# Recurrence and gated FFN on one core: weights converted without their range handling, and the range counted in a second pass

## The chip, the cores and the metric

The kernel runs on one core of one Trainium2 chip. The metric is device time in microseconds (us), from one launch. Five engines work side by side, each through its own list of instructions in order: TensorE (PE in the profile; its weight loads are PEld), VectorE (DVE), ScalarE (ACT), GpSimd (POOL) and SyncE (SP, which here only issues DMAs). Waits between engines are semaphores.

## The reference

A linear recurrence over 768 time steps for 4 batches and 8 heads of width 48, followed by a two-layer FFN over the resulting 3072 tokens of width 384. The gate is mish, written as `h * tanh(log1p(exp(h)))`.

```python
for t in range(S):                                   # r, k, v: (4, 8, 768, 48); w, u: (8, 48)
    cur = einsum('bhd,bhe->bhde', u[None] * k[:, :, t], v[:, :, t])
    y[:, :, t] = einsum('bhd,bhde->bhe', r[:, :, t], state + cur)
    state = w[None, :, :, None] * state + einsum('bhd,bhe->bhde', k[:, :, t], v[:, :, t])
x = y.transpose(0, 2, 1, 3).reshape(B * S, H * D)    # (3072, 384)
h = x @ w_in                                         # (384, 2048)
out = (h * tanh(log1p(exp(min(h, 20))))) @ w_out     # (2048, 384)
```

`w_in` and `w_out` arrive as float64, all else as float32. [...]

## The kernel before

**Stages.** Time is cut into 6 chunks of 128 steps; a chunk of one batch is a *step* s (24 steps, four for each chunk). For each step `scale` multiplies r and k by powers of the decay, `scores` (L476) makes the products of a chunk in the PSUM pair `pa`, `attend` (L495) masks them into `P` with a copy under a predicate, and `outputs` makes y (L510, L512 for the first chunk, L527 and L536 later) and the next state. `diag` makes the diagonal of P first (L452 on ACT or L454 on DVE). In the first chunk `keys` (L466) multiplies k by the table `TKn`, and L560 copies a part of v into `pre` for y.

The four steps of a chunk together feed one *group* g of the FFN: 512 tokens, 16 up tiles of 128 features (`hp`), the gate, and 16 down tiles that add into `acc`. The down tile n comes LAG = 6 tiles behind the up tile n. Tiles are numbered through all groups, n = 0 to 95. Group 0 multiplies in plain float32 (L791 for its first four up tiles in pieces of one step each, L716 for the other up tiles, L760 for the down tiles; three matmuls a tile). Groups 1 to 5 use weights and activations that are split in two parts (`w`, nine matmuls a tile, L694). An up tile leaves PSUM by a copy on DVE or ACT (L832 `hb`), two PSUM buffers `hp` take turns. For each pair of tiles ACT runs three activations with two table loads (L727, L730, L733), DVE multiplies (L738, L740), and L744 and L748 split the result.

**Weights.** There are 16 chunks of 768 weights a partition: eight of `w_in` (two up tiles each), eight of `w_out` (two down tiles each), in the order `W_ORDER` in which group 0 needs them: in 0 to 3, out 0, in 4, out 1, in 5, out 2, in 6 and so on. `load_weights` loads each as 768 KB of float64 (tile `wraw`) through POOL's queue. `convert(c)` turns it in place into float32: `up` and `low` are the two halves; the exponent is moved over by shifting `up` left by 3 (L316) after its sign is cleared (L308 on ACT, or L310 on DVE) and the value is clamped into the exponents that the shift can take (L312); the low half becomes a correction (L314 on ACT); the sign is put back (L318); the two are added (L320). `split(c)` (L333, L335) later makes the two parts for groups 1 to 5. Buffers of raw chunks and of parts share 17 slots (`W_SLOTS`).

**What sets the order.** `Flow` plans the whole program before it is emitted: each thread (`convert`, `gate`, `ffn` and so on) yields the events that it needs and the cost of its next instruction for each engine that could take it; `run` takes the one that is ready first, by rank. So the list of each engine is fixed by the planner's costs; where a thread yields costs for two engines (`hb`, `gh`, `diag`), the planner also chooses the engine. `check_range` counts the decays `w` that lie in the range that the kernel is made for, and the last lines load that count: if one is outside, a general path (slow, not run with these inputs) computes all again.

Of the kernel before, what the change touches and what calls it, by code (L numbers as in the profile page):

```python
# [36 lines left out]
E_LO, E_HI = (float(np.array([n], np.uint32).view(np.float32)[0]) for n in (896 << 20, (1151 << 20) - 1))  # L37
# [23 lines left out]
N_SQ = 4  # L61
N_ACT_DIAG = 8
# [74 lines left out]
def dve(cols, fast=False):  # L137
    return {"dve": 0.14 + cols / (1900 if fast else 950)}
# [6 lines left out]
def pe(us):  # L145
    return {"pe": us}
# [3 lines left out]
def rwkv_mish_kernel(ctx, tc, rkT, rkN, vN, wT, w_in, w_out, consts, rkF, vF, wF, uF, outT):  # L150
# [10 lines left out]
    small = const.tile([128, 4 * NP + 4], F32, name="small")  # L161
    wt, wc, iw, inr = (small[:, n * NP : (n + 1) * NP] for n in range(4))
    bias_ln2, early, ones = (small[:, 4 * NP + n : 4 * NP + n + 1] for n in range(3))
    ok = small[0:32, 4 * NP + 3 :].bitcast(I32)
# [100 lines left out]
    def check_range():  # L265
        yield "TKn"
        yield "state3"
        yield {"pool": 0.1}
        nc.gpsimd.memset(ones, 1.0)
        yield dve(NP)  # L270
        nc.vector.tensor_tensor(out=inr, in0=wc, in1=wt, op=ALU.is_equal)
        yield pe(0.1)
        t = ps.tile([128, 512], F32, name="ok", tag="acc2")
        nc.tensor.matmul(t[:32, :NP], lhsT=ones.broadcast_to([128, 32]), rhs=inr, start=True, stop=True)
        yield dve(NP)
        nc.vector.tensor_reduce(out=inr[:32, 0:1], in_=t[:32, :NP], axis=AX.X, op=ALU.add)
        yield dve(1)
        nc.vector.tensor_copy(ok, inr[:32, 0:1])
        flow.set("checked")
# [5 lines left out]

    def load_weights():
        for c, (i, f) in enumerate(W_ORDER):
            yield {"pool": 1.2}
            raws[c] = raw = wpool.tile([128, WE, 2], U32, name="wraw", tag="w")
            nc.gpsimd.dma_start(raw, (w_in, w_out)[i][f].bitcast(U32).rearrange("p (n two) -> p n two", two=2))  # L290
            flow.set(f"issued{c}")

    def convert(c):
# [10 lines left out]
        engine = yield {**dve(WE, True), **act(WE)}  # L304
        e = stage.tile([128, WE], F32, name="we", tag="we", bufs=2)
        eu = e.bitcast(U32)
        if engine == "act":
            nc.scalar.activation(e, up.bitcast(F32), AF.Abs)  # L308
        else:
            v.tensor_scalar(out=eu, in0=up, scalar1=0x7FFFFFFF, scalar2=None, op0=ALU.bitwise_and)  # L310
        yield dve(WE, True)
        v.tensor_scalar(out=e, in0=e, scalar1=E_LO, scalar2=E_HI, op0=ALU.max, op1=ALU.min)  # L312
# [770 lines left out]
```

## Time and profile before

| | |
|---|---|
| three timed runs | 523.43, 523.54, 521.80 us; median 523.43 |
| profiled execution | 521.48 us; span of its instructions 519.7 us |
| mean granted TensorE clock | 0.982 |
| busy share of the span | PE 96%, ACT 78%, DVE 72%, POOL 2% |
| DMA | 46.27 MB, 89 GB/s on average |

PE has hardly any time left over the whole span, but the three stages differ. Up to about 50 us the DMA queues are full with inputs and weights; from there to about 160 us group 0 runs, the weights are converted and split, and DVE and ACT are nearly as busy as PE; after that PE leads by a wide margin until about 512 us. The times of a line in the timeline are the start from the span's start and the duration; in the timeline each float32 matmul shows as two records, so six records are one tile of group 0. Next to a time in brackets stands how long the engine had been idle and what ended it; "issue" there means that the profile shows nothing that was waited for.

### The profile page before, as it was taken

The numbers are of one execution on the slowest core, as the hardware profiler recorded it, in microseconds if no ns is written. First come the engines' busy times: TensorE is split into PE (matmuls) and PEld (weight loads), VectorE is DVE, ScalarE is ACT, GpSimd is POOL, SyncE is SP. The second block draws the span as 40 slices with busy tenths as digits, with TensorE's granted clock in tenths as the row PEclk, the third lists the DMA queues.
The fourth block names the chain that finished last, engine by engine and source line by source line (L and its number), as shares of the span: only waits on it lengthen the run. The fifth ranks groups of instructions, "written<-read, shape, count | busy, mean of one in ns | idle before, by whom it ended". The sixth has DMA issues, their size and how long they took to land. (4 is left out here: it accounts for less than half of the span.)

```text
span 519.7 us, 8994 instructions
## 1 busy us (share of the span) xinstructions
PE 498.7 (96%) x3654; PEld 384.6 (74%) x3654; DVE 373.9 (72%) x582; ACT 404.1 (78%) x504; POOL 10.7 (2%) x25
## 2 busy tenths in 40 slices
PE   6988997999999999999999999999999999999994
PEld 4777462555658888887888888888888888888883
DVE  4949997999988897677966478857488545546551
ACT  2945999789987898876797987887978869769660
POOL 5110000000000000000000000000000000000000
PEclk8789998999999999999999999999999999999999
DMA  8999332211114312013412124321123000010001
GB/s 267 324 365 368 135 115 74 88 61 42 37 50 138 113 41 63 20 67 110 140 44 58 30 73 131 105 66 36 53 78 119 1 6 11 1 61 1 0 1 66
DMA packets 17138, 46.27 MB, mean 89 GB/s; under 512 B 2817, under 2 KB 3329, under 8 KB 17089
## 3 DMA queue, kind: packets, MB, share of 16 engines
q1 hardware_dynamic: 12048, 27.93, 17.8%
q0 software_dynamic: 2304, 12.58, 6.8%
q10 hardware_dynamic: 2736, 5.10, 2.7%
q8 instruction: 31, 0.51, 0.4%
q14 instruction: 19, 0.15, 0.1%
HBM read 38.92 MB, written 4.72 MB: 84 GB/s over the span
## 5 line engine op out<-in xcount | busy, mean ns | idle before, releaser
L694 PE MATMUL hp<-x,w 128*128 128x512 f32 x720 | 181.0, 396 | 0.8 <-DVE hb L832 0.6
L694 PE MATMUL acc<-gh,w 128*128 128x512 f32 x480 | 159.8, 389 | 0.0
L694 PEld LDWEIGHTS hp<-x,w 128*128 128x128 f32 x720 | 133.7, 188 | 32.4 <-issue 1.6
L694 PEld LDWEIGHTS acc<-gh,w 128*128 128x128 f32 x480 | 90.1, 188 | 18.8
L694 PE MATMUL acc<-gl,w 128*128 128x512 f32 x240 | 93.4, 389 | 0.0
L832 DVE COPY hb<-hp 128x512 f32<-128x512 f32 x48 | 33.1, 690 | 55.5 <-PE hp L694 51.3
L740 DVE TENSOR_TENSOR hb<-hb,fa 128x1024 f32<-128x1024 f32 x40 | 48.7, 1219 | 27.4 <-ACT fa L733 27.3
L727 ACT ACTIVATE fa<-hb,small 128x1024 f32<-128x1024 f32 x48 | 55.3, 1152 | 13.9 <-DVE hb L740 13.5
L727 ACT ACT_TABLE_LOAD x48 | 61.6, 1283 | 5.5 <-DVE hb L740 3.7
L733 ACT ACT_TABLE_LOAD x48 | 61.6, 1283 | 0.9
L694 PEld LDWEIGHTS acc<-gl,w 128*128 128x128 f32 x240 | 45.0, 188 | 9.4
L730 ACT ACTIVATE fa<-fa 128x1024 f32<-128x1024 f32 x48 | 50.9, 1060 | 1.0
L733 ACT ACTIVATE fa<-fa 128x1024 f32<-128x1024 f32 x48 | 50.9, 1060 | 0.5
L748 DVE TENSOR_TENSOR gl<-hb,gh 128x1024 fp32r<-128x1024 f32 x40 | 48.8, 1220 | 1.6 <-ACT gh L744 1.2
L832 ACT COPY hb<-hp 128x512 f32<-128x512 f32 x48 | 28.0, 583 | 22.3 <-PE hp L694 18.7
L760 PE MATMUL acc<-gf,wraw 128*128 128x512 f32 x96 | 44.0, 594 | 0.0
L716 PE MATMUL hp<-x,wraw 128*128 128x512 f32 x72 | 35.2, 627 | 3.7 <-issue 3.7
L495 DVE COPY_PREDICATED P<-cst,pa 128x512 f32<-128x512 uint32 x48 | 34.9, 728 | 3.2 <-PE pa L476 2.4
L744 ACT CAST gh<-hb 128x1024 fp32r<-128x1024 f32 x18 | 18.9, 1052 | 19.8 <-DVE hb L740 19.1
L760 PEld LDWEIGHTS acc<-gf,wraw 128*128 128x128 f32 x96 | 18.7, 196 | 19.2 <-issue 18.1
L402 DVE TENSOR_TENSOR rk<-rk,TRK 112x512 f32<-112x512 f32 x44 | 30.0, 683 | 0.0
L716 PEld LDWEIGHTS hp<-x,wraw 128*128 128x128 f32 x72 | 14.0, 201 | 19.4 <-issue 19.1
(101 smaller groups left out, 529.0 us busy)
## 6 DMA issues: line engine op xcount, KB each, us to landing
rk<-in_rkT_dram SPq DMA_DIRECT2D x22, 448.0 KB, 4.0
rkn<-in_rkN_dram SPq DMA_DIRECT2D x20, 384.0 KB, 3.8
wraw<-in_w_in_dram POOLq DMA_DIRECT2D x8, 768.0 KB, 21.7
wraw<-in_w_out_dram POOLq DMA_DIRECT2D x8, 768.0 KB, 23.0
v<-in_vN_dram SPq DMA_DIRECT2D x22, 256.0 KB, 4.0
out_dram<-ob ACTq DMA_DIRECT2D x18, 256.0 KB, 2.2
x<-st SPq DMA_DIRECT2D x60, 32.0 KB, 1.9
rkx<-in_rkT_dram SPq DMA_DIRECT2D x2, 448.0 KB, 16.7
```

The source lines that it names most:

```text
L402: nc.vector.tensor_tensor(out=rk[:112, a], in0=rk[:112, a], in1=TRK[:112, a], op=ALU.mult)
L495: nc.vector.copy_predicated(out=Ps[s][:, :, i].rearrange("j (w z) i -> j w z i", w=2), mask=masks.unsqueeze(2).broadcast_to([128, 2, NP // ...
L694: nc.tensor.matmul(out, lhsT=a, rhs=m, start=first and n == 0, stop=last and n == 2)
L716: nc.tensor.matmul(hp[:, :T], lhsT=e[:, fs], rhs=o.x[:, k, :, 0], start=k == 0, stop=k == KT - 1)
L727: nc.scalar.activation(o.g, o.hb, AF.Sigmoid, bias=bias_ln2, scale=1.0)
L730: nc.scalar.activation(o.g, o.g, AF.Arctan)
L733: nc.scalar.activation(o.g, o.g, AF.Sin, scale=2.0)
L740: nc.vector.tensor_tensor(out=o.hb, in0=o.hb, in1=o.g, op=ALU.mult)
L744: (nc.scalar.copy if engine == "act" else nc.vector.tensor_copy)(out=o.gh, in_=o.hb)
L748: nc.vector.tensor_tensor(out=o.gl, in0=o.hb, in1=o.gh.bitcast(F32), op=ALU.subtract)
L760: nc.tensor.matmul(a, lhsT=whole[1, f // WG][:, ws], rhs=o.gf[:, j], start=f == 0, stop=f == NF - 1)
L832: (nc.scalar.copy if engine == "act" else nc.vector.tensor_copy)(out=o.hb[:, j], in_=h)
```

## The change

`convert` loses its first two instructions: the sign is no longer cleared ahead of the shift (the shift by 3 pushes it out) and the clamp is gone. The shift (now at line 347) reads `up` of the raw chunk. What the clamp guarded is counted later: `check_range` starts after the last split, loads all 16 chunks a second time through SP's queue into the one free slot of the weight buffers, one every three up tiles from tile 44 on, squares the upper half on ACT with a sum (L291), takes the smallest square on DVE (L293), and folds both into `flags`. The one matmul that counts all flags moves from group 0 to just after up tile 92 and takes an `hp` buffer. The first down tile no longer waits for `checked`. The general path converts the weights anew with the clamp. Nothing is changed in what the kernel returns.

```diff
     def check_range():
-        yield "TKn"
-        yield "state3"
+        v = nc.vector
+        yield "w1,%d" % (NW - 1)
         yield {"pool": 0.1}
         nc.gpsimd.memset(ones, 1.0)
+        for c, (i, f) in enumerate(W_ORDER):
+            yield f"u{CHECK_AT + CHECK_STEP * c}"
+            yield {"sp": 2.0}
+            if not c:
+                raw = wpool.tile([128, WE, 2], U32, name="wraw", tag="w")
+            nc.sync.dma_start(raw, weights(c))
+            yield act(WE)
+            e = stage.tile([128, WE], F32, name="we", tag="we", bufs=2)
+            to = more if c else flags
+            nc.scalar.activation(e, raw[:, :, 1].bitcast(F32), AF.Square, accum_out=to[:, 1:2])
+            yield dve(WE)
+            v.tensor_reduce(out=to[:, 0:1], in_=e, axis=AX.X, op=ALU.min)
+            if c:
+                yield {"dve": 0.3}
+                for k, op in enumerate((ALU.min, ALU.add)):
+                    v.tensor_tensor(out=flags[:, k : k + 1], in0=flags[:, k : k + 1], in1=to[:, k : k + 1], op=op)
...
+        yield from hp_free()
+        yield pe(0.3)
+        yield from hp_free(0.0)
+        t = hp_tile("ok", "counted")
+        nc.tensor.matmul(t[:32, :N_FLAGS], lhsT=ones.broadcast_to([128, 32]), rhs=flags, start=True, stop=True)
...
     def convert(c):
...
-        engine = yield {**dve(WE, True), **act(WE)}
-        e = stage.tile([128, WE], F32, name="we", tag="we", bufs=2)
-        eu = e.bitcast(U32)
-        if engine == "act":
-            nc.scalar.activation(e, up.bitcast(F32), AF.Abs)
-        else:
-            v.tensor_scalar(out=eu, in0=up, scalar1=0x7FFFFFFF, scalar2=None, op0=ALU.bitwise_and)
-        yield dve(WE, True)
-        v.tensor_scalar(out=e, in0=e, scalar1=E_LO, scalar2=E_HI, op0=ALU.max, op1=ALU.min)
         yield act(WE)
         nc.scalar.activation(r, low, AF.Copy, bias=2.0, scale=2.0**-51)
         yield dve(WE, True)
-        v.tensor_scalar(out=eu, in0=eu, scalar1=3, scalar2=None, op0=ALU.logical_shift_left)
+        e = stage.tile([128, WE], F32, name="we", tag="we", bufs=2)
+        eu = e.bitcast(U32)
+        v.tensor_scalar(out=eu, in0=up, scalar1=3, scalar2=None, op0=ALU.logical_shift_left)
...
     def down_tile(n):
...
-                yield "checked"
...
-    flow.start(check_range(), -100, 0.0)
+    flow.start(check_range(), 999, 0.0)
...
-    with tc.If(in_range < 128 * NP):
+    with tc.If(in_range < 128 * N_FLAGS):
```

Since costs change, the planner writes nearly every engine's list anew from the first conversion on. Lines behind L308 of the kernel before have other numbers now: L314 is L345, L318 is L349, L320 is L351, L466 is L497, L495 is L526, L560 is L591, L727, L730 and L733 are L758, L761 and L764, L832 is L863. The numbers behind a name's underscore are buffers.

VectorE, group 0, the conversion of the chunk of `w_in` that up tiles 10 and 11 read (in 5; the raw buffer is wraw_223 before, wraw_222 now). Before, its last two instructions (L318 and L320 on wraw_223) stand behind the gate product of the third tile pair (`gf`) and work for the steps 5 and 6 (`yt`, `yh`, `x`, `rkn`, `P`); its shift comes just ahead of these rows:

```order
L738 TENSOR_TENSOR gf_869<-hb_599,fa_789 128x1024
L644 TENSOR_TENSOR x_750<-yh_809,x_750 128x128
L585 TENSOR_TENSOR S_77<-S_77,yt_808 48x192
L466 TENSOR_TENSOR rkn_779<-rkn_779,TKn_87 128x384
L644 TENSOR_TENSOR x_750<-yt_808,x_750 128x2x128
L495 COPY_PREDICATED P_861<-cst_70,pa0_92 128x4x128
L318 SCALAR_TENSOR_TENSOR we_756<-wraw_223,we_756 128x768
L495 COPY_PREDICATED P_861<-cst_70,pa1_93 128x4x128
L320 ISA wraw_223<-wraw_223,we_756 128x768x2
```

Now the chunk is converted whole, right behind the conversion of another (wraw_190), four rows ahead of the gate product of the first tile pair:

```order
L351 ISA wraw_190<-wraw_190,we_570 128x768x2
L347 TENSOR_SCALAR we_607<-wraw_222 128x768
L349 SCALAR_TENSOR_TENSOR we_607<-wraw_222,we_607 128x768
L433 TENSOR_TENSOR rk_591<-rk_591,TRK_86 112x512
L351 ISA wraw_222<-wraw_222,we_607 128x768x2
```

The chunk's last instruction moved from row 128 of VectorE's list to row 66, and the clamp is no longer among its rows; the tile pair that reads it is the sixth.

VectorE in the first stage, around the last of the four `kn` products (which wait for loads) and the masking of step 3 (the copies under a predicate from `pa`). Before:

```order
L466 TENSOR_TENSOR kn_164<-kn_164,TKn_87 128x384
L312 TENSOR_SCALAR we_324<-we_324 128x768
L495 COPY_PREDICATED P_428<-cst_70,pa0_92 128x4x128
L312 TENSOR_SCALAR we_409<-we_409 128x768
L495 COPY_PREDICATED P_428<-cst_70,pa1_93 128x4x128
L612 COPY S_77<-st_488 48x192
L560 COPY pre2_89<-vx_124 128x6x16
```

Now:

```order
L526 COPY_PREDICATED P_427<-cst_70,pa0_92 128x4x128
L497 TENSOR_TENSOR kn_164<-kn_164,TKn_87 128x384
L526 COPY_PREDICATED P_427<-cst_70,pa1_93 128x4x128
L347 TENSOR_SCALAR we_504<-wraw_160 128x768
L351 ISA wraw_156<-wraw_156,we_405 128x768x2
```

P_428 before and P_427 now are the masked products of step 3. Its first masking copy now precedes the last `kn` product, no conversion stands between the two copies, and the copy into `pre` of step 3 has moved to ACT.

ScalarE in the last third, around one of the new squares (L291), a row of the second pass:

```order
L863 COPY hb<-hp 128x512
L764 ACT_TABLE_LOAD
L764 ACTIVATE fa<-fa 128x1024
L291 ACTIVATE we,small<-wraw 128x768
L863 COPY hb<-hp 128x512
L775 CAST gh<-hb 128x1024
L758 ACT_TABLE_LOAD
```

The square stands between the gate of one tile pair and the copy of the next tile out of PSUM; over the whole program ACT now has 63 of the 96 `hb` copies instead of 48, and the count of table loads (97) is the same.

SyncE's queue near its end: the last seven loads of the second pass (`wraw`), and the two sets of six small DMAs that bring rows of `x` to their partitions for the last group (`x<-st`). Before, the two sets stood next to each other; now:

```order
L685 DMA x<-st_3391 16x512 x6
L287 DMA wraw<-in_w_in_dram 128x1536
L287 DMA wraw<-in_w_out_dram 128x1536
L287 DMA wraw<-in_w_in_dram 128x1536
L685 DMA x<-st_3681 16x512 x6
L287 DMA wraw<-in_w_out_dram 128x1536 x4
```

Each load of the second pass writes the same buffer, so it waits for the square of the one ahead, and what stands behind it in the queue waits with it.

More of the change, by code (lines that the diff above doesn't have):

```diff
@@ L35, with as_float @@
 NW = NF // WG
-E_LO, E_HI = (float(np.array([n], np.uint32).view(np.float32)[0]) for n in (896 << 20, (1151 << 20) - 1))
+def as_float(n):
+    return float(np.array([n], np.uint32).view(np.float32)[0])
+E_LO, E_HI = as_float(896 << 20), as_float((1151 << 20) - 1)
+A_LO, A_HI = as_float(898 << 20) ** 2, as_float(1149 << 20) ** 2
+N_FLAGS = 2 + NP
 ROWS = (slice(0, D), slice(64, 64 + D))
@@ L61 @@
 N_SQ = 4
+CHECK_AT, CHECK_STEP = 44, 3
 N_ACT_DIAG = 8
@@ L160, in rwkv_mish_kernel @@
     cst = const.tile([128, N_CST + 2 * NP + DM], F32, name="cst")
[L161 to L164, printed above, removed]
+    small = const.tile([128, 6 + 3 * NP + N_FLAGS], F32, name="small")
+    bias_ln2, early, ones = (small[:, n : n + 1] for n in range(3))
+    ok = small[0:32, 3:4].bitcast(I32)
+    wt, wc, iw = (small[:, 4 + n * NP : 4 + (n + 1) * NP] for n in range(3))
+    flags = small[:, 4 + 3 * NP : 4 + 3 * NP + N_FLAGS]
+    more = small[:, 4 + 3 * NP + N_FLAGS :]
     zeros = const.tile([128, 1], BF16, name="zeros")
@@ L275, in check_range, with weights @@
         yield dve(NP)
-        nc.vector.tensor_reduce(out=inr[:32, 0:1], in_=t[:32, :NP], axis=AX.X, op=ALU.add)
+        v.tensor_reduce(out=flags[:32, 0:1], in_=t[:32, :N_FLAGS], axis=AX.X, op=ALU.add)
         yield dve(1)
-        nc.vector.tensor_copy(ok, inr[:32, 0:1])
-        flow.set("checked")
+        v.tensor_copy(ok, flags[:32, 0:1])
+        flow.set("counted")
     W_ORDER = sorted(((i, f) for i in range(2) for f in range(NW)), key=lambda w: w[1] * WG + w[0] * W_SHIFT)
     raws, whole, parts = {}, {}, {}
+    def weights(c):
+        i, f = W_ORDER[c]
+        return (w_in, w_out)[i][f].bitcast(U32).rearrange("p (n two) -> p n two", two=2)
@@ L286, in load_weights @@
     def load_weights():
-        for c, (i, f) in enumerate(W_ORDER):
+        for c in range(len(W_ORDER)):
             yield {"pool": 1.2}
             raws[c] = raw = wpool.tile([128, WE, 2], U32, name="wraw", tag="w")
-            nc.gpsimd.dma_start(raw, (w_in, w_out)[i][f].bitcast(U32).rearrange("p (n two) -> p n two", two=2))
+            nc.gpsimd.dma_start(raw, weights(c))
             flow.set(f"issued{c}")
```

28 lines of the change are left out of this document (23 added, 5 removed).

## The prediction

> **What bounds the kernel now.** First the page's busy line, then the same by stages, because a share over the span hides where one engine leads.
>
> ```profile
> PE 498.7 (96%) x3654; PEld 384.6 (74%) x3654; DVE 373.9 (72%) x582; ACT 404.1 (78%) x504; POOL 10.7 (2%) x25
> ```
>
> By stages (each row: length; busy time of PE, PEld, DVE, ACT, POOL; granted TensorE clock; DMA share; GB/s):
>
> ```profile
> 32.80:36.60 3.80, 3.71 (x54) 3.60 (x55) 1.29 (x4) 1.08 (x2) 0.64 (x2) 0.55 1.04 342
> 39.90:42.80 2.90, 1.64 (x24) 1.29 (x22) 2.84 (x7) 0.00 (x0) 0.00 (x0) 1.00 1.03 387
> 42.80:49.90 7.10, 7.10 (x82) 6.71 (x81) 6.18 (x10) 5.72 (x10) 0.00 (x0) 1.00 1.02 358
> 49.90:82.80 32.90, 32.90 (x256) 17.29 (x254) 30.73 (x58) 32.68 (x57) 0.00 (x0) 1.00 0.36 128
> 82.80:86.70 3.90, 0.20 (x1) 0.03 (x1) 3.87 (x7) 3.87 (x6) 0.00 (x0) 1.00 0.12 25
> 86.70:91.10 4.40, 4.40 (x6) 1.44 (x6) 2.51 (x5) 4.37 (x6) 0.00 (x0) 0.61 0.54 171
> 91.10:124.70 33.60, 33.60 (x228) 17.82 (x227) 31.64 (x54) 28.42 (x41) 0.00 (x0) 1.00 0.21 64
> 160.00:510.00 350.00, 349.23 (x2395) 288.36 (x2394) 240.24 (x344) 275.27 (x298) 0.00 (x0) 1.00 0.18 56
> ```
>
> From 42.8 us on PE is never idle but in one place, 82.8 to 86.7, and the 4.4 us after it run at a granted clock of 0.61. In group 0 (49.9 to 124.7) DVE and ACT are over 84% busy, in the last 350 us 69% and 79%. The list of PE's waits says the same; after the first stage only these three are left:
>
> ```profile
> PE hp L716 <- issue: 3.7, 1, 3.7
> PE hp L694 <- DVE hb L832: 0.6, 1, 0.6
> PE hp L694 <- ACT hb L832: 0.2, 1, 0.2
> ```
>
> So the time is PE's work plus what delays PE's first full tile (up tile 4) plus this one stall. "issue" names nobody; the timeline around it does:
>
> ```profile
> 80.26 2.74 PE L760 MATMUL acc<-gf,wraw 128*128 128x512 f32 x6
> 86.70 4.51 PE L716 MATMUL hp<-x,wraw 128*128 128x512 f32 x6 [3.70 <-issue]
> 91.14 0.33 PE L527 MATMUL yt<-rk,S 48*64 48x128 f32 x2
> 85.66 0.94 DVE L320 CUSTOM_DVE_ANT_0 wraw<-wraw,we 128x1536 uint16<-128x1536 uint16 x1
> ```
>
> L320 ends at 85.66 + 0.94 = 86.60, and the up tile starts at 86.70. By the program's order this L320 finishes the weights that up tile 10 reads, the tile at 86.70. The stall is a conversion that comes late in DVE's list.
>
> **Term 1: the stall.** Where PE runs through, a tile of group 0 takes 101.62 - 99.05 = 2.57 us:
>
> ```profile
> 99.05 2.74 PE L760 MATMUL acc<-gf,wraw 128*128 128x512 f32 x6
> 101.62 2.74 PE L716 MATMUL hp<-x,wraw 128*128 128x512 f32 x6
> ```
>
> The down tile at 80.26 would have ended its turn at 82.83 and the up tile at 85.40; the next work began at 91.14. The stall costs 91.14 - 85.40 = 5.74 us: 3.87 idle and 1.87 of slow clock. What the conversions cost on the engines:
>
> ```profile
> L308 ACT ACTIVATE we<-wraw 128x768 f32<-128x768 f32 x13 | 11.8, 911 | 10.5 <-DMA wraw<-in_w_in_dram 9.0 <-DVE wraw L320 1.5
> L312 DVE TENSOR_SCALAR we<-we 128x768 f32<-128x768 f32 x16 | 8.8, 552 | 2.9 <-ACT we L308 2.9
> L310 DVE TENSOR_SCALAR we<-wraw 128x768 uint32<-128x768 uint32 x3 | 1.7, 555 | 0.0
> L316 DVE TENSOR_SCALAR we<-we 128x768 uint32<-128x768 uint32 x16 | 8.7, 550 | 0.0
> ```
>
> The edit removes L308, L310 and L312: 11.8 us of ACT and 10.5 us of DVE. The shift now reads every second word of the raw chunk instead of a dense tile; L310 reads the same words in 555 ns where the dense L316 takes 550, so that costs 16 x 5 ns = 0.1 us of DVE. More than these sums it is the order that counts: the conversion for tile 10 now stands at row 66 of DVE's list instead of 128, before the gate of the first tile pair. Counting the rows ahead of it at such durations from 39.2 (below), I put it near 51 us, some 30 us before the tile. The stall goes whole: -5.7 us. What is late next: DVE was still 94% busy from 91.1 to 124.7 and loses there only 0.55 us a chunk, so a later chunk or a mask could wait; and the first tile of a group has its `x` only about 2 us early (term 3). I take 0 for these and keep 0 to 5.7, the size of the one stall seen, for the range.
>
> **Term 2: the start.** Up tile 4 starts at 49.88, and what leads there is the masking of step 3, which stands in DVE's list behind a load:
>
> ```profile
> 29.83 0.56 DVE L466 TENSOR_TENSOR kn<-kn,TKn 128x384 f32<-128x384 f32 x1 [3.98 <-DMA kn<-in_rkN_dram]
> 32.12 0.71 DVE L495 COPY_PREDICATED P<-cst,pa 128x512 f32<-128x512 uint32 x1
> 37.95 0.56 DVE L466 TENSOR_TENSOR kn<-kn,TKn 128x384 f32<-128x384 f32 x1 [2.48 <-DMA kn<-in_rkN_dram]
> 39.97 0.71 DVE L495 COPY_PREDICATED P<-cst,pa 128x512 f32<-128x512 uint32 x1
> ```
>
> ```profile
> 37.16 2.39 PE L791 MATMUL hp<-x,wraw 128*128 128x128 f32 x18
> 41.38 0.32 PE L512 MATMUL yt<-P,pre 128*64 128x128 f32 x1 [1.26 <-DVE pre L560]
> 42.84 3.09 PE L791 MATMUL hp<-x,wraw 128*128 128x128 f32 x24
> 49.88 2.85 PE L716 MATMUL hp<-x,wraw 128*128 128x512 f32 x6
> ```
>
> The load of the last `kn` lands at 37.95 in any order: the DMA engines are full (share over 1.0 in the rows to 49.9) and what is queued ahead is unchanged. Now only one masking copy follows it: 37.95 + 0.56 + 0.71 = 39.2 instead of 39.97 + 0.71 = 40.7, and the copy into `pre`, for which PE waited until 41.38, is early on ACT. So y of step 3 goes on from 39.2, 2.2 us before 41.38. In PE's new order 18 matmuls of the early pieces are left after it instead of 24; 12 of them (24 records) take 3.09 us, so 6 take 1.5. Against that PE waits, by estimate, 0.3 us longer for ACT's copy of that y. At full clock up tile 4 comes 2.2 + 1.5 - 0.3 = 3.4 us earlier.
>
> But PE runs dry ahead of 39.2. Step 2's masks, behind the first `kn` before, are now ahead of it: from 25.85, where the wait of 3.98 began, eight instructions of a chunk's conversion and of masking (5 us) lead to 30.9. PE then still has 12 pieces of steps 0 and 1 until near 32, and what followed the masks before (32.83 to 37.16 + 2.39 = 39.55, less 1.7 of slow clock and 0.8 for three pieces done earlier) takes 4.2: PE is done near 36.2 and waits 3.0 us. After 3.9 us of idling the clock was at 0.61 for 4.4 us, 32.8 to 36.6 ran at 0.55 behind shorter gaps, and the 1.26 us before 41.38 had no effect. 3.0 is nearer to the first two, and 3.8 us at 0.55 lose 1.7. So -3.4 + 1.7 = -1.7; the ends are -3.4 and 0 (a longer slow stretch, or a mask later than in this chain).
>
> The Trainium skill (TensorE: Matmul & The Clock Gate, Part 1: The HAM clock gate) says that the array falls to half clock after at least one idle window of about 3.4 us and needs about as long busy to rise again. The 3.9 us gap and the 4.4 us at 0.61 agree; the 0.55 at 32.8, with no gap of 3.4 us ahead of it, does not fit so plainly. By that rule a gap of 3.0 us costs nothing and the term would be -3.4, the total 1.7 us lower.
>
> **Term 3: the second pass.** Each of its 16 rounds is a 768 KB load on SP's queue, a square on ACT (L308 is its shape: 911 ns), a reduction on DVE and from the second round on two tiny operations. Nearest rows for the reduction, the copies and the load:
>
> ```profile
> L437 DVE TENSOR_REDUCE sd<-rkn 128x8 f32<-128x384 f32 x20 | 11.0, 549 | 0.3
> L318 DVE SCALAR_TENSOR_TENSOR we<-wraw,we 128x768 uint32<-128x768 uint32 x16 | 15.1, 950 | 0.0
> L832 ACT COPY hb<-hp 128x512 f32<-128x512 f32 x48 | 28.0, 583 | 22.3 <-PE hp L694 18.7 <-PE hp L716 2.4 <-PE hp L791 1.1
> rk<-in_rkT_dram SPq DMA_DIRECT2D x22, 448.0 KB, 4.0
> x<-st SPq DMA_DIRECT2D x60, 32.0 KB, 1.9
> ```
>
> 384 elements are reduced in 549 ns; at 768 elements L318 takes 950, so I take 0.95 us, and 0.15 to 0.2 for each tiny one. On ACT the pass adds 16 x 0.91 = 14.6 us; the planner also moves 15 `hb` copies there from DVE, at 583 ns each 8.7 us more at most. In 160 to 510 ACT has 350 - 275.3 = 74.7 us idle and DVE 109.8, against 23.3 and about 20: both stay below PE. The sum of the squares leaves ACT with the same instruction (no row shows this form; 0.2 us more each would be 3.2 of the idle time). I book 0 to PE, with +0.5 for a few late `hb` copies as the two that PE waited for before (0.6 and 0.2); ends 0 and 5 (below). The counting matmul costs PE 0.2 us here as it did in group 0: 0. It waits for the last round; by the order that round's square stands in ACT's list a whole gate (L758 to L764) ahead of the copy of up tile 92, and the matmul comes after this tile, so it is ready.
>
> A load can also be in the way of others. From 32 and 448 KB the slope is 416 KB in 2.1 us, so 768 KB land in about 5.6 us. SP's queue holds `rk`, `rkn`, `v` and the `x` rows that the next group's first tile needs:
>
> ```profile
> 276.10 3.67 SPq L654 DMA_DIRECT2D x<-st  x6
> 283.53 2.20 PE L694 MATMUL hp<-x,w 128*128 128x512 f32 x9
> ```
>
> The last of the six lands at 276.10 + 3.67 + 1.9 = 281.7, 1.9 us ahead of up tile 48. A load of the second pass right in front would eat that. Since it waits only for the square before it and not for the tile that the planner named, it is out a tile or two earlier than planned, so I book 0.
>
> **Sum.** -5.7 - 1.7 + 0.5 = -6.9 us on the profiled execution's 521.48 us (519.7 of span and 1.8 around it): 514.6. The median of the runs, 523.43, lies 1.95 above it; I carry that over: 523.43 - 6.9 = 516.5.
>
> **The rivals.**
> - *The stall comes back elsewhere in group 0.* Its DVE stays near 90% busy, and one place of waiting can follow another. For it: the 94% row. Against it: PE ran through that row before. It gives back up to 5.7: 522.2, or 519.4 for half.
> - *The clock stays up at the start.* A gap of 3.0 us may be too short to lower it: for it the 1.26 us ahead of 41.38, against it the 0.55 row. Term 2 is then -3.4: 514.8. (It is what the clock gate's rule in the Trainium skill, above, gives.)
> - *The `x` rows wait behind a load.* The load takes 5.6 - 1.9 = 3.7 us more than a small one; less the margin of 1.9 that is 1.8 at each of the three group changes in the second pass, +5.4: 521.9.
> - *Slower: the squares hold ACT.* ACT takes its list in order; a square whose load is late holds the `hb` copies behind it. PE can go on for three tiles of at most 2.2 us (down, up, down), 6.6 us, before it needs the buffer. It ends above 523.43 + 2.6 only if 16 squares cost PE (6.9 + 2.6)/16 = 0.6 us each, that is, wait 7.2 us each; at 8 us it is 16 x 1.4 - 6.9 = +15.5: 538.9. For it: one buffer for all loads; against it: each load may start a whole round (three up and three down tiles, 12 to 13 us) ahead, and lands in 5.6.
>
> The Trainium skill (DMA: Bandwidth & Descriptors, Anatomy of one DMA) gives about 2 us fixed and 436 GB/s; by this 768 KB land in an estimated 3.8 us, below my 5.6, which would weaken the last two.
>
> **How the numbers follow.** Both terms as booked (514 to 518.5): 0.57. Clock stays up (513 to 514.8): 0.12. Stall elsewhere: 0.15, of which 0.09 within half of it and still faster. `x` rows: 0.10, 0.03 of it faster by only one late group. Squares hold ACT: 0.06. A difference under 0.5% (2.6 us, 520.8 to 526) can hardly be told from none. Faster: 0.57 + 0.12 + 0.09 + 0.03 = 0.81; same: 0.06 + 0.07 = 0.13; slower 0.06. The range goes from 513.0 (the start at its end and nothing lost, 514.3, with a median up to 1.3 lower, since the three runs spread by 1.7) to 521.0, which leaves out the slow case and the full sizes of the two middle rivals.
>
> **What would show it.** Right: no PE wait over 1 us after 50 us; up tile 4 near 48.2 and the first L725 tile near 117.3 (124.7 before); three DVE instructions a chunk; the squares at 0.9 us with ACT below 85% in the last 350 us. Wrong: a new row in PE's waits in group 0 (rival one), waits at up tiles 48, 64 or 80 (rival three), or ACT idle before L291 for the load (the last). If the conversions weren't what PE waited for at 86.70, that gap stays.

## The result and the profile after

The changed kernel takes 517.91 us (median of 4 runs, 516.7 to 519.62), the kernel before 523.48 us beside it: a ratio of 0.9895, 95% interval 0.9848 to 0.9942. A second set of 6 runs gave 518.26 us and 0.9885 (0.984 to 0.993). The profiled execution took 519.62 us, with a span of 517.7. It is the slowest of its four, while the profiled execution before lay 1.95 us below its median. So the two profiles stand only 2.0 us apart where the medians stand 5.6 apart. The stages show where the time went, and they come first.

The page's busy line of the changed kernel, and four rows of its list of PE's waits (us in total, times, longest):

```profile
PE 498.6 (96%) x3656; PEld 385.2 (74%) x3656; DVE 371.1 (72%) x591; ACT 418.2 (81%) x536; POOL 10.8 (2%) x25
```

```profile
PE yt L543 <- DVE P L526: 2.3, 1, 2.3
...
PE hp L725 <- DVE hb L863: 2.2, 1, 2.2
...
PE acc L725 <- DVE gl L779: 0.8, 1, 0.8
PE acc L725 <- DVE gh L775: 0.5, 1, 0.5
```

The wait of 3.7 us on "issue" ahead of up tile 10 is gone, and so are the two waits of 0.6 and 0.2 for `hb` copies. New are the wait of 2.2 us for an `hb` copy on DVE and the two small ones for `gl` and `gh`. By stages (length; busy time of PE, PEld, DVE, ACT, POOL; granted clock; DMA share; GB/s):

```profile
36.60:39.90 3.30, 0.97 (x9) 0.64 (x9) 1.40 (x3) 0.46 (x1) 0.00 (x0) 0.97 1.02 289
39.90:42.80 2.90, 2.90 (x35) 2.89 (x36) 2.90 (x5) 0.10 (x1) 0.00 (x0) 0.50 1.01 385
...
82.80:86.70 3.90, 3.90 (x11) 1.80 (x10) 3.81 (x9) 3.70 (x7) 0.00 (x0) 1.00 0.29 94
86.70:91.10 4.40, 4.40 (x12) 2.04 (x11) 4.40 (x9) 3.11 (x5) 0.00 (x0) 1.00 0.35 92
...
160.00:510.00 350.00, 346.52 (x2373) 285.11 (x2372) 239.56 (x367) 293.83 (x340) 0.00 (x0) 1.00 0.28 89
```

PE is full and at full clock from 82.8 to 91.1, where it had 0.20 us of work and then a clock of 0.61. In the last 350 us ACT is busy for 293.83 us (84%) instead of 275.27, and PE for 346.52 instead of 349.23. Three starts of up tiles give the steps: tile 4, tile 16 (the first of group 1) and tile 95 (the last).

```profile
48.23 2.32 PE L747 MATMUL hp<-x,wraw 128*128 128x512 f32 x5
117.63 1.73 PE L725 MATMUL hp<-x,w 128*128 128x512 f32 x5
492.50 2.20 PE L725 MATMUL hp<-x,w 128*128 128x512 f32 x9
```

Read for every tile and set against the kernel before (49.88, 124.68 and 496.27 for these three), the difference in the profiled executions grows like this, in us; "again" is a second profile of the same changed kernel, "conversion alone" is explained below:

| stretch | changed | again | conversion alone |
|---|---|---|---|
| up to tile 4 (start) | -1.65 | -3.40 | -3.47 |
| tile 4 to 16 (the stall of before) | -5.40 | -5.40 | -5.20 |
| tile 16 to 54 (the two small waits of before) | -1.22 | -1.18 | -1.18 |
| tile 54 to 57 | +4.11 | +4.27 | 0 |
| the count, near tile 90 or 92 | +0.38 | +0.39 | +0.39 |
| from tile 95 to the end | +1.8 | +2.1 | -0.2 |
| span against 519.7 | -2.0 | -3.2 | -9.7 |

By tile 54 the changed kernel is 8.3 us ahead in the first profile and 10.0 in the second (9.9 with the conversion alone). Two places far behind the conversion then took 6 back.

### The profile page after: what moved, and what is told of

It is laid out like the page before. It is cut to its first block, busy times and chain, and to the rows that moved or that the text cites. A ratio compares the mean times of both kernels' runs of the same rounds, so it can differ in the third digit from the quotient of the medians.

```text
span 517.7 us, 9047 instructions
## 1 busy us (share of the span) xinstructions
PE 498.6 (96%) x3656; PEld 385.2 (74%) x3656; DVE 371.1 (72%) x591; ACT 418.2 (81%) x536; POOL 10.8 (2%) x25
## 3 DMA queue, kind: packets, MB, share of 16 engines
q1 hardware_dynamic: 14352, 40.51, 25.2%
## 5 line engine op out<-in xcount | busy, mean ns | idle before, releaser
L863 ACT COPY hb<-hp 128x512 f32<-128x512 f32 x63 | 36.9, 586 | 24.8 <-PE hp L725 20.8
L758 ACT ACTIVATE fa<-hb,small 128x1024 f32<-128x1024 f32 x48 | 55.3, 1153 | 0.6
L761 ACT ACTIVATE fa<-fa 128x1024 f32<-128x1024 f32 x48 | 50.9, 1060 | 1.0
L764 ACT ACTIVATE fa<-fa 128x1024 f32<-128x1024 f32 x48 | 50.9, 1061 | 0.5
L863 DVE COPY hb<-hp 128x512 f32<-128x512 f32 x33 | 22.8, 690 | 22.1 <-PE hp L725 20.6
L526 DVE COPY_PREDICATED P<-cst,pa 128x512 f32<-128x512 uint32 x48 | 34.8, 731 | 2.9 <-ACT P L483 1.5
L775 ACT CAST gh<-hb 128x1024 fp32r<-128x1024 f32 x21 | 22.1, 1053 | 17.7 <-DVE hb L771 16.8
L747 PE MATMUL hp<-x,wraw 128*128 128x512 f32 x72 | 33.5, 602 | 0.0
L343 ACT ACTIVATE wraw<-wraw 128x768 f32<-128x768 uint32 x16 | 14.6, 927 | 12.4 <-DMA wraw<-in_w_in_dram 12.4
```

The source lines that it names most:

```text
L526: nc.vector.copy_predicated(out=Ps[s][:, :, i].rearrange("j (w z) i -> j w z i", w=2), mask=masks.unsqueeze(2).broadcast_to([128, 2, NP // ...
L747: nc.tensor.matmul(hp[:, :T], lhsT=e[:, fs], rhs=o.x[:, k, :, 0], start=k == 0, stop=k == KT - 1)
L758: nc.scalar.activation(o.g, o.hb, AF.Sigmoid, bias=bias_ln2, scale=1.0)
L761: nc.scalar.activation(o.g, o.g, AF.Arctan)
L764: nc.scalar.activation(o.g, o.g, AF.Sin, scale=2.0)
L775: (nc.scalar.copy if engine == "act" else nc.vector.tensor_copy)(out=o.gh, in_=o.hb)
```

## The experiments

Each ratio is to the kernel before, timed on the same chip in the same rounds. Rows one to four, five to eight and nine to twelve come from three chips, on which the kernel before took 523.42, 521.62 and 522.87 us; so rows of different sets are compared by their ratios.

| kernel | median us | ratio, 95% interval | span of the profile |
|---|---|---|---|
| changed, again | 518.26 | 0.9885 (0.984 to 0.993) | 516.5 |
| conversion alone | 513.15 | 0.979 (0.9745 to 0.9834) | 510.0 |
| pass of 4 columns | 518.53 | 0.989 (0.9841 to 0.994) | 515.1 |
| old order, without the work | 519.89 | 0.9927 (0.9896 to 0.9959) | 518.6 |
| pass free of planned cost | 517.49 | 0.9924 (0.9899 to 0.9949) | 514.3 |
| two output copies on DVE | 514.58 | 0.9871 (0.9845 to 0.9898) | 511.7 |
| old work, earlier order | 548.93 | 1.0527 (1.0501 to 1.0552) | 546.6 |
| pass alone | 535.82 | 1.0272 (1.0237 to 1.0307) | 535.6 |
| count moved | 530.43 | 1.0128 (1.0076 to 1.0179) | 528.4 |
| conversion with the old count | 513.57 | 0.9824 (0.9782 to 0.9866) | 510.4 |
| one copy on ACT | 521.06 | 0.9963 (0.994 to 0.9986) | 519.7 |
| output copies on DVE, warm start | 515.66 | 0.9871 (0.983 to 0.9911) | 513.8 |

### The wait before up tile 55: chance, work or order

**The changed kernel again.**

> The changed kernel once more, unaltered. In its profile PE waited 2.2 us before up tile 55 for a copy into hb on DVE, and ran about 2 us slower behind it: some 4.1 us. Theory A (the order of the lists makes this wait: three output copies of group 2 stand on ACT, the third waits for an output transfer, and the hb copy of tile 54 stands on DVE behind rows that wait for ACT): the wait of about 2 us before up tile 55 is in this profile too. Theory B (a transfer that came late by chance in one execution): no wait before up tile 55 in this profile, and its span is about 4 us shorter, near 513.6. The median time is 517 to 519 by both.

The wait is there again (2.40 us), and from tile 54 to 57 the loss is 4.27 us. It is no chance of one execution. The timeline of the first profile shows the chain, here ACT, ACT's queue, SP's queue, DVE and PE (start, length, engine and line):

```profile
303.65 0.57 ACT L798 COPY ob<-acc 128x512 f32<-128x512 f32 x1
304.25 0.34 ACTq L799 DMA_DIRECT2D out_dram<-ob  x1
304.63 0.59 ACT L798 COPY ob<-acc 128x512 f32<-128x512 f32 x1 [0.41 <-ACT ob L798]
...
307.82 0.59 ACT L798 COPY ob<-acc 128x512 f32<-128x512 f32 x1 [2.60 <-DMA out_dram<-ob]
...
308.81 0.27 ACT L673 CAST st<-yh 128x128 fp32r<-128x128 f32 x1 [0.41 <-ACT ob L798]
308.98 1.05 ACT L775 CAST gh<-hb 128x1024 fp32r<-128x1024 f32 x1
```

```profile
303.45 0.33 SPq L404 DMA_DIRECT2D rk<-in_rkT_dram  x1
```

```profile
309.11 0.29 DVE L675 TENSOR_TENSOR st<-yh,st 128x128 fp32r<-128x128 f32 x1 [3.20 <-ACT st L673]
309.32 0.34 DVE L616 TENSOR_TENSOR S<-S,yt 48x192 f32<-48x192 f32 x1
310.06 1.23 DVE L779 TENSOR_TENSOR gl<-hb,gh 128x1024 fp32r<-128x1024 f32 x1 [0.41 <-ACT gh L775]
311.20 0.68 DVE L863 COPY hb<-hp 128x512 f32<-128x512 f32 x1
```

```profile
311.94 3.54 PE L725 MATMUL hp<-x,w 128*128 128x512 f32 x9 [2.18 <-DVE hb L863]
```

Read it backwards. Up tile 55 needs the PSUM buffer that the `hb` copy of tile 54 empties, because `yh` holds the other one. That copy stands on DVE behind `gl`, which needs `gh` from ACT. On ACT, `gh` and the cast into `st` stand behind the third copy of group 2's output, and this one waits 2.60 us for a transfer out of one of the only two `ob` buffers. Before the change two of the three output copies were on DVE. The planner, charging ACT and DVE for the second pass, put all three on ACT; without that charge two are on DVE again (the pass free of planned cost, below).

**The pass on 4 columns, in the same order.**

```diff
-            nc.scalar.activation(e, raw[:, :, 1].bitcast(F32), AF.Square, accum_out=to[:, 1:2])
+            nc.scalar.activation(e[:, :4], raw[:, :4, 1].bitcast(F32), AF.Square, accum_out=to[:, 1:2])
...
-            v.tensor_reduce(out=to[:, 0:1], in_=e, axis=AX.X, op=ALU.min)
+            v.tensor_reduce(out=to[:, 0:1], in_=e[:, :4], axis=AX.X, op=ALU.min)
```

> The changed kernel in exactly its own order of instructions, but the squares and the reductions of the second pass work on 4 of 768 columns (only these are checked); the 768 KB loads stay. About 13 us of ACT and 13 us of DVE go. Theory A (order): the wait before up tile 55 stays at about 2 us and the time within 1 us of the changed kernel, 517 to 518.5. Theory D (the squares and reductions hold ACT and DVE up, so that the hb copy is late): the wait goes and the time falls by about 4 us, to 513.5 to 514.5.

The wait stays at 2.2 us with nearly no work in the pass (below), and the median is that of the changed kernel. So it is the order and not the squares and reductions. The 768 KB loads stay in this kernel; the pass free of planned cost (below) has them too, and no wait at tile 55. In the profile the pass on 4 columns loses 2.52 us from tile 54 to 57 instead of 4.1 to 4.3, because the clock stayed up behind the gap. The same up tile in five kernels (9 matmuls; behind a gap at full clock they take 2.34):

```profile
310.46 3.91 PE L725 MATMUL hp<-x,w 128*128 128x512 f32 x9 [2.40 <-DVE hb L863]
```

```profile
310.79 2.34 PE L725 MATMUL hp<-x,w 128*128 128x512 f32 x9 [2.23 <-DVE hb L863]
```

```profile
330.22 2.33 PE L732 MATMUL hp<-x,w 128*128 128x512 f32 x9 [2.50 <-DVE hb L870]
```

```profile
313.86 3.23 PE L725 MATMUL hp<-x,w 128*128 128x512 f32 x9 [3.16 <-ACT hb L863]
```

These are the changed kernel again, the pass on 4 columns, the pass alone and the one copy on ACT (the last two are below); the fifth is the row of 311.94 above. A gap of 2.2 to 2.5 us brought the slow clock in two executions and not in two others; the last section shows what made the difference.

**The conversion alone.**

```diff
-        for c, (i, f) in enumerate(W_ORDER):
-            yield f"u{CHECK_AT + CHECK_STEP * c}"
...
+        nc.gpsimd.memset(flags[:, :2], 1.0)
+        yield f"u{CHECK_AT + CHECK_STEP * 15}"
```

> The new conversion alone: the second pass over the weights (loads, squares, reductions) is left out, so the range of the weights isn't looked at. The two terms of the conversion without the pass. Theory A: with the planner's order free of the pass, two of the three output copies of group 2 go to DVE as before the change and the hb copy of tile 54 goes to another place; no wait at up tile 55, and the kernel is about 8 us below the one before: 515.4, 2.5 to 4 below the changed kernel. Theory C (the pass costs PE nothing and the missing microseconds were lost by the conversion's own new order): within 1 us of the changed kernel, 517 to 519. Up tile 4 near 48.2 and the first tile of group 1 near 117.6 by both.

It is faster than expected: 513.15 us, 5.1 below the changed kernel in the same rounds. The third output copy stands there too, but two of the three copies are on DVE, as before the change, and the transfers ahead of the third left earlier:

```profile
300.61 0.34 ACTq L781 DMA_DIRECT2D out_dram<-ob  x1
...
302.73 0.59 ACT L780 COPY ob<-acc 128x512 f32<-128x512 f32 x1 [0.56 <-DMA out_dram<-ob]
...
308.02 2.20 PE L707 MATMUL hp<-x,w 128*128 128x512 f32 x9
```

No wait at tile 55 (308.02). It also shows what was not in anyone's expectation: the end. From the start of tile 95 to the end of the span the changed kernel takes 517.7 - 492.50 = 25.2 us, this one 510.0 - 486.80 = 23.2, the kernel before 519.7 - 496.27 = 23.4, and the pass on 4 columns 25.4. With the pass in its plan ACT has the last `hb` copies of up tiles, which ran on DVE before, and the last gates come late; the waits of 0.8 and 0.5 us for `gl` and `gh` in the list above are at this place. The work of the pass is over by then (the count's matmul of the changed kernel runs at 482.0), and the end is as long with the pass on 4 columns, so this too is order.

**Two output copies held to DVE.**

```diff
     def output(g, mt):
-        engine = yield {**dve(T), **act(T)}
+        engine = yield dve(T) if (g, mt) in ((2, 0), (2, 1)) else {**dve(T), **act(T)}
```

> The changed kernel with its planned costs, but the first two output copies of group 2 are held to DVE, as they stood before the change; the rest is planned anew around them, and the hb copy of tile 54 comes to stand on ACT. Theory A (late output copies on ACT are what the chain to up tile 55 begins with): the third output copy waits about 0.6 us for an output transfer instead of 2.6 to 2.8, the wait before up tile 55 goes, and the time falls to 513.5 to 514.5. Theory F (the hb copy waits whichever engine has it, now behind a square and a gate copy on ACT): a wait of 1 to 2 us stays, 516 to 518.

It takes 514.58 us, and there is no wait before up tile 55: tile 54 starts at 303.34 and tile 55 at 307.58, one tile later. The way was not quite the one written down: the third copy, now on DVE, still waits 2.50 us, and ACT with it, since ACT issues its transfer. But the output leaves earlier against tile 54, and the `hb` copy of this tile, right behind the gate's cast on ACT, starts 3.2 us after the tile (306.57 - 303.34) instead of 5.8 (311.20 - 305.37). The end still takes 511.7 - 486.36 = 25.3 us; that loss is untouched.

**One copy on ACT.**

```diff
-        engine = yield {**dve(o.T), **act(o.T)}
+        engine = yield act(o.T) if n == 54 else {**dve(o.T), **act(o.T)}
```

> The changed kernel with only the hb copy of tile 54 held to ACT; the three output copies of group 2 stay on ACT. Theory A (the chain begins with the late output copies): the third of them waits 2.6 to 2.8 us for an output transfer as before, and the hb copy, behind the gate's cast, a table load and the sigmoid on ACT, ends about 1.2 us later than it did on DVE (1.05 + 1.28 + 1.15 + 0.59 us behind 308.98 against 311.88): a wait of 3 to 3.5 us before up tile 55, 518.5 to 520. Rival (the copy's place behind the gate's rows on DVE is the cause): the wait goes, 513.5 to 514.5.

The wait is 3.16 us, inside the 3 to 3.5 worked out from the rows on ACT, and the median is 521.06, 1 us above the range. So moving the `hb` copy alone makes it worse: the chain begins at the output copies.

**The pass free of planned cost.**

```diff
-            yield {"sp": 2.0}
+            yield {"sp": 0.0}
...
-            yield act(WE)
+            yield {"act": 0.0}
...
-            yield dve(WE)
+            yield {"dve": 0.0}
...
-                yield {"dve": 0.3}
+                yield {"dve": 0.0}
```

> The changed kernel with all work of the second pass, but the planner is told that the pass's loads, squares, reductions and small operations cost no time. So it no longer gives other work a different engine on their account: two output copies of group 2 go to DVE again and the hb copies are those of the conversion alone, but for one. Theory A (the pass's true work is hidden; only the order that the planner made for it cost time): no wait at up tile 55, and the time is that of the conversion alone plus the 0.4 us of the counting matmul, 513.2 to 514.2. Theory E (without planned room the squares hold the hb copies behind them on ACT): waits of 0.3 us or more at many of the 16 rounds, 515 to 519.

It takes 517.49 us: theory A misses by 3 us, and theory E has the time but not its many waits of 0.3 us or more. There is no wait at tile 55 and the end takes 514.3 - 490.98 = 23.3 us, as it should by A. But one wait of 1.84 us came at up tile 71, in the next group, by the same chain: the DVE copies of the output are behind the pass's small operations, and their transfers leave together with the step's loads.

```profile
380.34 1.85 ACTq L799 DMA_DIRECT2D out_dram<-ob  x2
...
384.70 0.59 ACT L798 COPY ob<-acc 128x512 f32<-128x512 f32 x1 [3.92 <-DMA out_dram<-ob]
```

```profile
380.37 0.33 SPq L404 DMA_DIRECT2D rk<-in_rkT_dram  x1
```

The other 1.9 us against the conversion alone lie at the start (up tile 4 at 48.37 instead of 46.41), where the executions of one kernel differ by as much. In the times there is no gain over the changed kernel (0.9924 against 0.9885), so what this run shows is where the two losses come from, and not a better kernel.

### The stall before up tile 10: work or order

**The old order, without the work.**

```diff
-            nc.scalar.activation(e, up.bitcast(F32), AF.Abs)
+            nc.scalar.activation(e[:, :1], up.bitcast(F32)[:, :1], AF.Abs)
...
-            v.tensor_scalar(out=eu, in0=up, scalar1=0x7FFFFFFF, scalar2=None, op0=ALU.bitwise_and)
+            v.tensor_scalar(out=eu[:, :1], in0=up[:, :1], scalar1=0x7FFFFFFF, scalar2=None, op0=ALU.bitwise_and)
...
-        v.tensor_scalar(out=e, in0=e, scalar1=E_LO, scalar2=E_HI, op0=ALU.max, op1=ALU.min)
+        v.tensor_scalar(out=e[:, :1], in0=e[:, :1], scalar1=E_LO, scalar2=E_HI, op0=ALU.max, op1=ALU.min)
...
-        v.tensor_scalar(out=eu, in0=eu, scalar1=3, scalar2=None, op0=ALU.logical_shift_left)
+        v.tensor_scalar(out=eu, in0=up, scalar1=3, scalar2=None, op0=ALU.logical_shift_left)
```

> The kernel before in exactly its own order of instructions, but the absolute value and the clamp work on 1 of 768 columns (weights below or above the range are not clamped), and the shift reads the raw words. This takes away the work that the change removes, some 11 us of ACT and 7 us of DVE, and keeps the order. Theory P (of the prediction: the order counts more than the work, the conversion of chunk 5 stands too late in DVE's list): only about 0.4 to 0.5 us on DVE for each of the chunks 2 to 5 comes off before up tile 10, so its wait falls from 3.9 to about 2 us and the time by 2 to 3 us, to 520.5 to 521.5. Rival W (the work itself): the wait goes whole, and the time falls by about 6 to 7 us, to about 517.

```profile
85.79 4.51 PE L716 MATMUL hp<-x,wraw 128*128 128x512 f32 x6 [2.84 <-issue]
```

```profile
84.74 0.95 DVE L320 CUSTOM_DVE_ANT_0 wraw<-wraw,we 128x1536 uint16<-128x1536 uint16 x1
```

The conversion's last step comes 0.91 us earlier (85.69 instead of 86.60), the wait falls from 3.70 to 2.84, and the slow clock behind it stays (six matmuls in 4.51 us). Taking the work away in place is worth 0.9 us of the 5.4, less than expected. By the medians it is worth 3.5 us; the profiles show no place for the other 2.6, and the profiled execution before was 1.95 below its own median. Where they lie is open.

**The old work, in an earlier order.**

```diff
-        flow.start(convert(c), (-999.5, -998.5)[c] if c < 2 else f * WG
+        flow.start(convert(c), (-999.5, -998.5)[c] if c < 2 else -16 + f * WG
```

> The kernel before with its old conversion, absolute value and clamp and all, but each conversion from chunk 2 on ranks 16 tiles earlier with the planner; the last step of the chunk that up tile 10 reads stands at row 89 of DVE's list instead of 128. Theory P (the order made the stall at up tile 10): the wait of 3.7 us and the slow clock behind it go with all the work still there, 517.4 to 518.5. Rival W (DVE has too much work in group 0): the wait moves to another tile of group 0 or stays, 521 or more.

It is 27 us slower. The conversions now stand ahead of gates, and PE waits for the gates instead:

```profile
PE acc L760 <- DVE gf L738: 15.9, 2, 9.8
```

So my theory as stated (the order alone makes the stall) falls. Neither half does it: the lighter work in the old place gains 0.9 us, and an earlier place with the old work moves the stall. What the change has is both: with 10.5 us of DVE and 11.8 us of ACT gone the same ranks give a list in which the conversions are early and the gates are not late. This experiment moves all 14 later chunks by 16 tiles; a finer ranking of the old conversion was not tried. Nor was it tried apart whether the removed cost moves the conversions in the list, or only that each has two steps fewer.

### The rest of the change

**The pass alone.** The kernel has the old lines of the conversion and the new `check_range`.

> The second pass alone: the old conversion with the absolute value and the clamp stays, and the pass of the changed kernel is added with its planned costs. The planner puts three output copies of group 2 on ACT and the hb copy of tile 54 behind rows that wait for ACT, as in the changed kernel. Theory A: the wait of 2.2 to 2.4 us before up tile 55 appears, with the slow clock behind it in most executions; the pass costs 4 to 5 us, 527.5 to 528.5. If the wait came from the conversion's new order instead: no wait at up tile 55, 523 to 524.5.

**The count moved.** As the pass alone, without the loop over the chunks.

> The old conversion with the absolute value and the clamp, no second pass; of the change only the place of the count is kept (after up tile 89 instead of in group 0, so the first down tile no longer waits for it). The second pass with the old conversion was 14 us slower than the kernel before, 10 more than its wait at up tile 55: PE waited 4.8 and 3.4 us in group 0, where the pass issues nothing. Theory G (moving the count makes the planner list group 0 anew, and with the old conversion's work there DVE comes late): the same waits of about 4.8 and 3.4 us stand in group 0 without any pass, 530 to 533. Rival H (the pass's planned costs do it): no new wait in group 0, 522 to 525.

The pass alone is 14 us slower, three times what was expected, and the count moved shows that a good half of it (7.6 us by the medians, 8.7 of 15.9 in the profiles) is not the pass. PE's waits with the count moved:

```profile
PE hp L736 <- DVE wraw L340: 4.8, 1, 4.8
...
PE hp L736 <- issue: 3.4, 1, 3.4
```

These two waits are in group 0, the same as with the pass. One count taken out of group 0 makes the planner list its DVE work anew, and with the old conversion's work that list has two late conversions. Between the two kernels the profiles differ by 1.0 us when group 0 is past its waits, by 3.7 behind up tile 55 (so 2.7 there, its clock stayed up) and by 535.6 - 528.4 = 7.2 at the end.

**The conversion with the old count.** The kernel before with the new lines of `convert` only.

> The new conversion with the count where it was before the change, in group 0; no second pass, the range of the weights isn't looked at. Its list is that of the conversion alone but for the few rows of the count. Theory: the conversion carries the gain by itself, and moving the count is worth nothing beside it: within 1 us of the conversion alone, 9 to 10 us below the kernel before, 512.5 to 514.5. Rival: the gain needs the count out of group 0: a wait of 1 us or more in group 0, 516 or more.

It takes 513.57 us, 0.9824 (0.9782 to 0.9866): with the new conversion the place of the count is worth nothing that can be measured.

**The warm start.**

```diff
     def scores(s):
         rk = loaded[s][0]
+        if s == 2:
+            keep_warm(8, pa[0][:, :256])
...
         y = ps.tile([128, 512], F32, name="yt", tag="yt")
+        if s == 3:
+            keep_warm(8, y[:, :256])
```

> The version with two output copies of group 2 held to DVE, and 16 matmuls of zeros (0.11 us each) more at the start: 8 ahead of the scores of step 2, 8 ahead of y of step 3, the two places where PE waited 0.8 to 1.9 and 2.3 us in the profiles and ran at half clock behind. Theory S (a slow stretch behind these gaps costs up to 1.9 us in some executions): up tile 4 starts at 46.0 to 46.5 in every execution (46.0 to 48.4 in the profiles so far), no row with a granted clock below 0.9 between 33 and 48 us, and the median falls by 0.5 to 1 us, ratio to the kernel before 0.985 to 0.986 (0.987 without them). Rival: the clock there has another reason, or the matmuls are in the way: up tile 4 at 47 or later, ratio 0.987 to 0.99.

In the profile the start goes as theory S says: the gap ahead of y of step 3 is 0.87 us, the clock stays at 1.00 and up tile 4 starts at 45.73.

```profile
36.60:39.90 3.30, 2.43 (x31) 1.93 (x30) 2.36 (x4) 0.07 (x1) 0.00 (x0) 1.00 1.01 298
39.90:42.80 2.90, 2.90 (x41) 2.85 (x38) 2.90 (x5) 2.29 (x5) 0.00 (x0) 1.00 1.01 398
```

That the added matmuls did it is not shown: the conversion with the old count, which has none, ran from 20 to 45 us at a clock of 1.00 too and started up tile 4 at the same 45.73. The ratio is the same 0.9871 as without, so no gain in the time is shown. In this execution the chain of the output copies struck at another group's change: the third copy of group 0's output waited 3.67 us for a transfer, and PE 2.11 us for an `hb` copy behind it.

```profile
147.11 0.35 ACTq L803 DMA_DIRECT2D out_dram<-ob  x1
...
151.76 0.59 ACT L802 COPY ob<-acc 128x512 f32<-128x512 f32 x1 [3.67 <-DMA out_dram<-ob]
```

## Why the prediction was right, and where it was not

The median is 517.9 us against 516.5 predicted (513.0 to 521.0), faster by 1.0%. The stall and the start came out as reasoned, in the main. That the total lies so near is luck: the second pass cost PE over ten times what was booked, and a distance between profile and median that did not last hid it. By steps:

- **Term 1, the stall.** Right in place and size: -5.40 measured from tile 4 to 16 (-5.74 predicted). Up tile 16 started at 117.63 (117.3 predicted), and the conversion that up tile 10 reads ended at 51.97 + 0.95 = 52.9 (near 51 predicted). The reason given was half right. "More than these sums it is the order that counts" holds for the work in place (0.9 us), but the one earlier order that was tried with the old work was far slower (548.93).
- **Term 2, the start.** -1.65 in the first profile (-1.7 predicted), up tile 4 at 48.23 (48.2 predicted), with a gap of 2.33 us instead of 3.0 and a clock of 0.50 behind it. That it fits to 0.1 us is luck in part: y of step 3 went on at 39.84 and not at 39.2, and the 0.5 us of `st` products of step 3, which stood ahead of up tile 4 before, now stand behind it (50.91), which was not in the sum; nor did the 0.3 us of waiting for ACT's copy come. The other value, -3.4, is just as real: -3.40 in the second profile of the changed kernel and -3.47 in that of the conversion alone. In the first of these (rows below) the slow stretch came earlier, and PE's backlog filled the gap. So this term has no one size; over the profiles of all versions with the new conversion it goes from -0.8 (one copy on ACT, up tile 4 at 49.12) to -4.15 (45.73).

```profile
30.00:33.00 3.00, 3.00 (x18) 2.78 (x15) 2.58 (x5) 2.58 (x7) 0.53 (x1) 0.50 1.02 404
37.30:39.50 2.20, 1.99 (x30) 1.81 (x25) 2.20 (x4) 2.02 (x5) 0.00 (x0) 1.00 1.04 290
```

- **Term 3, the second pass.** This is the term that was mis-sized. Booked was +0.5 "for a few late `hb` copies"; measured are +4.1 to 4.3 at tile 55, +0.4 for the count (booked at 0) and +1.8 to 2.1 at the end: 6.3 to 6.8, above the upper end of 5 that was kept. Against it stand -1.2 from tile 16 to 54, where the two small waits of before went away; no term named them, and since the conversion alone has the same -1.18 they are not the pass's. It was right that the squares cost PE nothing (904 ns each, as said) and wrong to look only at how late a copy would be by the pass's work. The planner's new places for copies that have nothing to do with the pass cost more than ten times the booked half microsecond.

The groups of the pass itself (line, engine, operation, count; busy time, mean ns; idle time ahead) and the landing of its loads:

```profile
L291 ACT ACTIVATE we<-wraw 128x768 f32<-128x768 f32 x16 | 14.5, 904 | 2.4 <-DVE ob L798 1.2 <-DMA wraw<-in_w_in_dram 1.2
L291 ACT ACTIVATION_READ_ACCUMULATOR we<-wraw 128x1 f32 x16 | 3.1, 195 | 0.0
L293 DVE TENSOR_REDUCE small<-we 128x1 f32<-128x768 f32 x16 | 15.2, 949 | 5.2 <-ACT we L291 5.2
```

```profile
wraw<-in_w_in_dram SPq DMA_DIRECT2D x8, 768.0 KB, 4.4
```

The squares, the reductions (949 ns, 0.95 predicted) and the tiny operations are as sized; reading the sum out costs the 0.2 us each that was left open. The loads land in 4.4 us, between my 5.6 and the 3.8 estimated from the Trainium skill (DMA: Bandwidth & Descriptors, Anatomy of one DMA). The Trainium skill fits these figures there to transfers issued from GpSimd, and the loads of the pass are issued from SyncE, so the estimate carries them over to another path.

The other rivals did not come: there was no stall elsewhere in group 0; no wait at up tiles 48, 64 or 80, so the `x` rows did not come late behind a load; the squares waited 1.2 us for loads in all. The sign that was to show the forecast right, "no PE wait over 1 us after 50 us", failed: the wait of 2.18 us at tile 55 is the one that no rival named.

- **The sum.** The terms as measured give -2 (first profile) to -3 (again) on the profiled execution, not -6.9. The median came out near the forecast because a second step failed the other way, which is luck: I carried over the 1.95 us by which the profiled execution before lay below its median, and after the change there is no such distance (518.28 profiled against a median of 518.26, again). Why most executions of the kernel before are slower than the profiled one is open.

Of the versions that do the whole computation, the one with two output copies on DVE has the lowest ratio, 0.9871 (0.9845 to 0.9898), the same as with the warm start. Its interval overlaps that of the changed kernel (0.9885, 0.984 to 0.993). So the 4 us at tile 55 are shown by the profiles (no loss from tile 54 to 57, against 4.1 and 4.3), not by the times. The conversion alone says what is left: about 2 us at the end.

## What to carry to other kernels

Where a planner chooses engines, work that fits into idle time is not free: its planned cost moves other work, and a copy that stands in a list behind one wait can hold PE at a place the new work never touches. So compare the two orders for the work that was *not* changed, above all where a buffer has only two slots, and test a suspected piece by shrinking it in place while its planned cost stays. Work and order are to be tried apart, and neither result promises the other.

## What the runs showed of the hardware

- *Slow clock behind short gaps.* Gaps of 2.18 and 2.40 us were followed by the slow clock (up tiles of 3.54 and 3.91 us), gaps of 2.23 and 2.50 us were not (2.34 and 2.33). The difference is where a gap lies. In every trace the granted clock changes only at times that lie a multiple of 3.41 us apart: in the changed kernel at 39.69, 43.10, 312.75 and 316.17, which is 1, 79 and 1 times 3.413 us. Cut into these periods, the changed kernel had its whole gap in one, and the next ran at 0.50; the pass on 4 columns had its gap of 2.23 split over two, with 1.27 and 0.96 us idle, and the clock stayed up:

```profile
309.34:312.75 3.41, 1.23 (x6) 0.68 (x5) 2.94 (x6) 3.38 (x5) 0.00 (x0) 1.00 0.22 84
312.75:316.16 3.41, 3.41 (x10) 2.64 (x9) 2.09 (x5) 3.38 (x6) 0.00 (x0) 0.50 0.02 5
```

```profile
306.42:309.83 3.41, 2.14 (x10) 1.44 (x8) 1.47 (x3) 2.73 (x4) 0.00 (x0) 1.00 0.55 210
309.83:313.24 3.41, 2.45 (x11) 2.03 (x12) 2.64 (x7) 3.38 (x8) 0.00 (x0) 1.00 0.00 0
```

Behind 50 us this holds in all fourteen profiles: each period at full clock in which PE was idle for 2.06 us or more was followed by the slow clock, and none with 1.83 us or less was. In the first stage this idle time alone doesn't decide it: there 0.84 us were enough once (the changed kernel again, near 24 us). The Trainium skill (TensorE: Matmul & The Clock Gate, Part 1: The HAM clock gate) asks for an idle window of about 3.4 us, and says that the window runs freely. The second agrees with these periods; the first is too strict for them, since 2.06 of 3.41 us idle were enough here.
- *An output transfer beside a load.* The third output copy of a group is released when the group's first output transfer has landed. From the issue of that transfer to the third copy it took 302.73 - 300.61 = 2.1 us where the step's 448 KB load of `rk` followed 1.3 us later (conversion alone), and 307.82 - 304.25 = 3.6 where the load went out 0.8 us ahead (changed kernel). With the load at most 0.2 us behind, both came: 4.4 and 4.65 us in two cases (384.70 - 380.34 and 151.76 - 147.11), but 149.78 - 147.36 = 2.4 in the version with two output copies on DVE, at the same copy of group 0 and with the same 0.21 us as in the second case. What decides there is not shown. The Trainium skill (DMA: Bandwidth & Descriptors, Queues, rings and completion order) says that each of the 16 DMA engines goes round between the queues that have work, packet by packet; a transfer that lands later beside a load fits that, but no row here shows the turns of one engine.
